# Sparse attention and a rational feed-forward layer on one core: four batches with padded values and DMA transposes, and a new written-out instruction order

## The chip, the core and the metric

The kernel runs on one core of one Trainium2 chip. Its time is device microseconds of one execution. The kernel before has a median of 383.21 us over 9 runs (381.69 to 384.72).

A core has engines that work side by side, each through its own list of instructions in a fixed order: PE (matrix products and transposes into PSUM), DVE (elementwise), ACT (activation functions and copies), POOL (here it issues the DMAs that cast float32 to bfloat16) and SP (issues all other DMAs, among them DMA transposes and the stores of the output). An engine that waits for a semaphore holds up all that is behind it in its list.

## The reference, cut to what matters

```python
def _attn_ref(q, k, v):                       # (8, 8, 576, 64)
    scores = matmul(q, k.transpose(0, 1, 3, 2)) / sqrt(64)
    rel = pos[:, None] - pos[None, :]
    mask_local = (rel >= 0) & (rel < 32)      # heads 0 to 3
    mask_strided = (rel >= 0) & (pos[None, :] % 32 == pos[:, None] % 32)   # heads 4 to 7
    attn = softmax(where(mask, scores, -1e9))
    return matmul(attn, v)

def _moe_ref(x, w_in, w_out, a, b):           # x: (4608, 512), w_in: (512, 2048)
    h = x @ w_in
    P = a[0] + a[1] * h + a[2] * h**2 + a[3] * h**3
    Q = 1.0 + abs(b[0]) * abs(h) + abs(b[1]) * h**2
    return (P / (Q + 1e-6)) @ w_out
```

The attention output, with its heads side by side, is x. Products run in bfloat16 with float32 sums.

## The kernel before, in words

**Attention by batch.** For each of 8 batches q and k are loaded in three parts (`load_qk`, L463: part 0 heads 4 to 7, part 1 heads 0 to 3, part 2 the last 64 positions in a tile tm), and v in three (`load_v`, L484: part 0 VL for the local heads, four DMAs on POOL and two copies on SP; part 1 VT for the strided heads, two DMAs; part 2 VW for the last positions). For batches from 2 on there is one VL, one VT and one VW buffer. They come free (`v_free`) when the last AV tile of the batch before has run.

`scores` (L625) makes, in steps: R1 transposes q and k of the strided heads (16 PE transposes, L680) and DVE copies the result into sT (L683); R2 and R3 do the same for the local heads into kL and qL (ACT); S and L are the scores of the strided and the local heads, whose exponentials ACT writes to ES and EL; TL is a DMA transpose of tm on SP; X holds the scores of the last positions, with exponentials in EX and EW. A branch with `name == "T"` makes sT by four DMA transposes on SP instead of R1, for batches from TB on; TB is 8 here, so no batch takes it.

`attend` (L787) makes five tiles for each batch, T0 to T4. Its matmuls (here called AV, L845) multiply the exponentials by v into 64 columns, and a matmul by ONE, a column of ones, puts the softmax's sum into column 64. For the local heads and VW the ones stand in the value tile itself, in column 64 of runs of VS = 68. DVE then takes the reciprocal of the sum (L853) and scales (L855) into XR. A transpose puts XR into XT, the input of the dense part: for the first four tiles of batches 0 and 1 by PE and a copy (L873, L875), for the others by a DMA transpose on SP (L885).

**Dense part by chunk.** Chunks 0 to 7 are the 512 first positions of each batch, chunk 8 the last 64 of all batches. `dense1` (L907) makes the first product (M1: groups of 8 matmuls 128x512), copies it to HB (ACT, L947), and computes the rational function: DVE L961 to L1012, ACT Ln and Exp (L985, L988) for the division. `dense2` (L1041) makes the second product with Wout (M2: for each chunk two halves, i0 and i1, of four groups of 8 matmuls) and stores. Win comes in four DMAs, Wout in one of 2 MB (L460), all on POOL.

**Order.** Nothing is left to the order of the code. `Program.schedule` (L169) gives each operation the rank that stands for it in the list ORDER, and each engine runs its operations by rank. `emit` puts in the waits. The costs and keys that `add` is given aren't used at run time. Fillers (L584) are matmuls without use, at ranks of their own.

**Batch 0.** Its q, k and v come by DMAs on SP as float32 (`loads0`, L527). DVE and ACT cast them; VL gets its three shifted copies from DVE (L558), ACT (L558) and POOL (L559).

```python
        for eng, o0, i0, n in (("DVE", 64, 64, 64), ("ACT", 32, 64, 32)):
            evl.append(evac(eng, VL[0][o0:o0 + n, 0:8, :, 0:64], stv[i0:i0 + n, :, :, :], [ovs, vi], -960, 2048))
```

Most matmuls are recorded under L597 and most PE transposes under L600, the lines of two helpers (`mm`, `tp`), so a reader goes by tile names.

Of the kernel before, what the change touches and what calls it, by code (L numbers as in the profile page):

```python
# [15 lines left out]
def _bf16_bits(x):  # L16
# [7 lines left out]
    0, 2, 1, 19, 3, 127, 71, 72, 73, 116, 33, 86, 99, 156, 153, 83, 110, 78, 105, 114, 34, 17, 98, 101, 109,  # L24
    12, 103, 36, 140, 82, 53, 108, 117, 97, 61, 25, 43, 118, 100, 50, 18, 112, 26, 60, 48, 29, 87, 55, 32,
    52, 23, 11, 104, 49, 51, 22, 30, 85, 35, 41, 56, 28, 84, 107, 59, 57, 44, 94, 81, 37, 119, 10, 62, 31,
    115, 111, 21, 141, 42, 15, 46, 45, 14, 40, 66, 79, 4, 27, 6, 58, 7, 68, 5, 38, 9, 13, 16, 8, 20, 24, 92,
    91, 93, 102, 77, 90, 132, 139, 65, 54, 39, 122, 47, 126, 63, 69, 70, 113, 75, 160, 158, 147, 154, 157,
    159, 67, 76, 74, 80, 64, 89, 88, 96, 95, 106, 123, 130, 131, 133, 136, 120, 124, 125, 143, 146, 135,
    142, 144, 148, 151, 129, 134, 138, 145, 150, 152, 170, 173, 178, 197, 207, 216, 221, 240, 121, 137, 162,  # L30
    164, 171, 194, 184, 202, 188, 179, 182, 198, 191, 175, 208, 149, 128, 204, 236, 239, 215, 211, 301, 299,
    229, 303, 193, 206, 228, 234, 225, 237, 238, 242, 243, 245, 161, 168, 174, 181, 183, 192, 200, 186, 190,
    195, 196, 203, 210, 155, 163, 165, 166, 169, 213, 232, 172, 176, 189, 217, 231, 241, 177, 187, 167, 180,
    201, 214, 223, 249, 256, 227, 235, 244, 246, 254, 283, 199, 209, 185, 205, 219, 226, 212, 220, 233, 250,
    292, 357, 375, 312, 341, 300, 307, 315, 322, 393, 398, 252, 258, 260, 263, 272, 255, 262, 264, 269, 273,
    265, 270, 274, 278, 280, 257, 268, 277, 281, 285, 230, 267, 275, 302, 287, 324, 333, 337, 343, 224, 222,
    251, 253, 261, 259, 282, 286, 290, 266, 271, 247, 276, 248, 294, 291, 279, 218, 318, 319, 306, 311, 313,
    320, 316, 296, 460, 284, 289, 293, 298, 304, 310, 314, 323, 327, 334, 309, 339, 345, 350, 355, 342, 347,
    348, 354, 353, 359, 360, 363, 365, 369, 370, 374, 373, 376, 378, 380, 381, 389, 390, 400, 288, 295, 297,
    305, 331, 335, 340, 382, 402, 351, 362, 372, 383, 386, 414, 308, 326, 317, 329, 406, 434, 438, 459, 479,  # L40
    448, 468, 494, 498, 514, 518, 330, 371, 356, 366, 377, 388, 384, 395, 410, 418, 426, 436, 503, 472, 521,
    442, 457, 483, 488, 501, 536, 325, 321, 328, 361, 336, 344, 346, 352, 349, 332, 338, 358, 364, 368, 392,
    396, 385, 387, 425, 427, 403, 405, 435, 409, 445, 415, 367, 379, 391, 397, 404, 412, 420, 429, 439, 444,
    394, 421, 451, 466, 464, 449, 452, 453, 458, 461, 463, 465, 469, 470, 473, 475, 478, 477, 480, 482, 484,
    485, 534, 548, 578, 407, 416, 399, 408, 424, 432, 413, 422, 441, 454, 431, 447, 462, 489, 456, 467, 507,
    523, 527, 567, 581, 552, 558, 543, 551, 574, 587, 612, 624, 535, 554, 557, 563, 580, 593, 603, 634, 541,
    549, 555, 559, 562, 615, 597, 599, 608, 568, 576, 590, 598, 604, 701, 669, 703, 670, 411, 428, 401, 455,
    417, 430, 437, 446, 443, 423, 419, 440, 433, 450, 491, 495, 487, 493, 547, 550, 505, 502, 513, 510, 515,
    544, 471, 476, 481, 486, 490, 492, 497, 500, 504, 509, 474, 496, 512, 516, 519, 564, 570, 571, 573, 575,
    577, 579, 611, 583, 589, 591, 594, 595, 600, 601, 605, 606, 655, 660, 693, 506, 511, 517, 528, 532, 546,  # L50
    525, 531, 553, 556, 561, 565, 585, 592, 538, 560, 613, 621, 627, 674, 677, 654, 702, 640, 645, 688, 729,
    713, 734, 635, 656, 663, 675, 694, 709, 717, 744, 609, 618, 628, 643, 662, 672, 762, 691, 668, 667, 679,
    705, 719, 725, 791, 761, 765, 790, 499, 508, 533, 530, 545, 539, 524, 526, 529, 537, 522, 542, 520, 540,
    626, 620, 617, 629, 651, 653, 614, 610, 647, 642, 657, 641, 566, 572, 584, 586, 588, 596, 602, 607, 616,
    619, 582, 623, 625, 630, 632, 676, 681, 683, 686, 687, 690, 692, 697, 698, 706, 708, 721, 711, 715, 716,
    718, 723, 742, 776, 795, 633, 646, 650, 665, 673, 682, 638, 648, 689, 696, 700, 710, 714, 720, 658, 671,
    724, 732, 737, 803, 814, 788, 810, 752, 758, 775, 825, 830, 838, 750, 769, 778, 797, 807, 827, 832, 856,
    730, 740, 755, 764, 785, 789, 802, 823, 826, 793, 813, 821, 831, 835, 839, 899, 842, 907, 569, 637, 631,
    652, 622, 666, 684, 644, 636, 659, 639, 661, 649, 664, 731, 733, 735, 728, 759, 757, 738, 739, 766, 743,
    774, 771, 678, 685, 695, 699, 704, 707, 712, 722, 727, 745, 726, 749, 753, 770, 772, 784, 792, 794, 798,  # L60
    799, 804, 805, 808, 812, 815, 816, 819, 818, 822, 824, 828, 837, 872, 873, 876, 736, 741, 747, 767, 773,
    781, 780, 796, 786, 800, 806, 820, 829, 833, 801, 809, 836, 844, 848, 888, 912, 879, 901, 864, 866, 921,
    929, 933, 942, 862, 875, 880, 892, 913, 925, 930, 946, 846, 858, 870, 877, 886, 904, 905, 900, 898, 889,
    897, 928, 931, 939, 962, 966, 943, 963, 779, 680, 783, 787, 751, 782, 754, 760, 777, 746, 748, 768, 763,
    756, 852, 847, 841, 843, 874, 868, 855, 850, 861, 857, 863, 859, 811, 817, 834, 845, 851, 854, 867, 878,
    881, 883, 869, 884, 887, 895, 910, 885, 890, 891, 893, 894, 902, 903, 916, 906, 909, 911, 914, 918, 922,
    923, 926, 964, 983, 985, 994, 840, 849, 853, 860, 865, 871, 915, 919, 882, 896, 908, 917, 920, 927, 924,
    932, 935, 938, 941, 965, 974, 953, 976, 949, 951, 968, 998, 993, 1002, 947, 954, 957, 969, 973, 979,
    986, 1006, 944, 948, 950, 952, 958, 992, 991, 997, 961, 970, 972, 977, 980, 984, 1015, 987, 1012, 988,
    934, 937, 940, 945, 955, 960, 936, 956, 967, 971, 975, 978, 982, 990, 959, 981, 995, 1000, 1001, 1034,  # L70
    1043, 1020, 1039, 1013, 1017, 1051, 1060, 1026, 1037, 1007, 1021, 1023, 1030, 1036, 1041, 1046, 1067,
    989, 996, 999, 1003, 1005, 1011, 1014, 1009, 1008, 1016, 1019, 1022, 1025, 1028, 1054, 1029, 1033, 1056,
    1004, 1018, 1027, 1032, 1042, 1045, 1010, 1024, 1050, 1055, 1058, 1074, 1085, 1081, 1095, 1062, 1064,
    1080, 1091, 1096, 1100, 1048, 1059, 1065, 1071, 1076, 1082, 1084, 1099, 1110, 1087, 1088, 1105, 1108,
    1112, 1121, 1089, 1093, 1098, 1103, 1104, 1106, 1119, 1113, 1116, 1118, 1130, 1143, 1145, 1035, 1047,
    1094, 1127, 1133, 1137, 1142, 1136, 1139, 1141, 1146, 1148, 1150, 1031, 1038, 1040, 1044, 1049, 1053,
    1073, 1072, 1075, 1052, 1057, 1061, 1063, 1066, 1068, 1077, 1079, 1069, 1070, 1078, 1083, 1086, 1090,
    1124, 1123, 1135, 1126, 1092, 1097, 1101, 1102, 1115, 1132, 1131, 1128, 1120, 1107, 1109, 1111, 1114,
    1117, 1122, 1125, 1129, 1134, 1138, 1140, 1144, 1147, 1149, 1151, 1152, 1153, 1159, 1157, 1156, 1155,
    1154, 1158, 1160, 1162, 1161  # L80
# [203 lines left out]
def bass_strided_sparse_attn__then__act_rational_pade_kernel(nc, q, k, v, moe_w_in, moe_w_out, moe_a, moe_b, out):  # L284
# [12 lines left out]
    HL, DA, TB, NF0 = 4, 1, 8, 70  # L297
# [18 lines left out]
    ES = [A(f"ES{i}", [128, 2, 512], BF) for i in range(NE)]  # L316
    EL = [A(f"EL{i}", [128, 2, 512], BF) for i in range(NE)]
    EX = [A(f"EX{i}", [128, 2, 64], BF) for i in range(NE)]
    EW = [A(f"EW{i}", [128, 12, 2, 32], BF) for i in range(NE)]
# [11 lines left out]
    VL = [A("VL0", [128, 9, 4, VS], BF)]  # L331
    VT = [A("VT0", [128, 4, 256], BF)]
    VW = [A("VW0", [128, 2, VS], BF)]
    t3f = T3[2].rearrange("x f c -> x (f c)")
    VL.append(t3f[:, 0:36 * VS].rearrange("x (m h d) -> x m h d", m=9, h=4))
    VW.append(t3f[:, 36 * VS:38 * VS].rearrange("x (j d) -> x j d", j=2))
    VT.append(t3f[:, 38 * VS:38 * VS + 1024].rearrange("x (h c) -> x h c", h=4))
    NU = 2
    UU = [A(f"UU{i}", [128, G, CH], BF) for i in range(NU)]
    NO = 2  # L340
    OS = [A(f"OS{i}", [128, 2, 512], F32) for i in range(NO)]
    Win = A("Win", [128, NK1, Fmid], BF)
    Wout = A("Wout", [128, NF, Fout], BF)
# [86 lines left out]
    for i in range(NE):  # L430
        memset(EW[i], EW[i].rearrange("x u j c -> x (u j c)"), 0.0, cost=0.5, key=-400 + 200 * i)
# [717 lines left out]
```

The softmax here doesn't subtract the row's maximum and nothing guards it: scores larger than these inputs give would overflow.

## Time and profile before

| what | value |
|---|---|
| median of 9 runs | 383.21 us |
| the profiled execution | 383.18 us |
| its span, first to last instruction | 381.4 us |
| granted PE clock, mean | 0.928 of full |
| dense matmuls 128x512, psO<-Wout | 512, 116.8 us busy in all |
| DVE copies sT<-psS | 8, 1.21 us each |
| matmuls by ONE (ES and EW) | 432 and 128 |
| POOL issues of VT | 12, 0.62 to 2.40 us, median 0.67; landing 4.6 us |
| POOL issues of VL | 24, 0.73 to 2.41 us, median 0.77; landing 3.5 us |
| SP issues of DMA transposes XT<-XR | 24, 1.19 to 4.35 us, median 1.25; landing 2.3 to 14.5, median 3.6 us |

One execution is profiled. Busy time is the time in which an engine runs an instruction; issuing a DMA isn't counted for SP. "Landing" is from the issue to the semaphore. "issue" as a releaser means that the engine waited for nothing that the profile shows. The slices are 40 equal parts of the span of 9.5 us each, with the busy share in tenths. The clock that the throttle grants PE is in tenths too.

### The profile page before, as it was taken

To read this page: it belongs to the slowest core of one execution; us is meant where nothing else is said; L and a number is where in the kernel's file an instruction comes from. 1 tells how busy PE (TensorE), PEld (TensorE's weight loads), DVE (VectorE), ACT (ScalarE), POOL (GpSimd) and SP (SyncE) were. 2 spreads that over 40 slices of the span, in tenths; PEclk is the share of its full clock that TensorE was granted. 3 is DMA by queue.
4 is the path that set the end of the run, shared out by engine and by line. 5 is a ranking of instruction groups with operands and counts; after the bars stand their busy time and mean duration, and the time that the engine had idled before them with its cause. 6 is when DMAs were issued, how large, how long until landed. Compare 5 with 4: busy or idle time off the path is not lost.

```text
span 381.4 us, 10809 instructions
## 1 busy us (share of the span) xinstructions
PE 335.2 (88%) x4902; PEld 178.0 (47%) x4902; DVE 319.6 (84%) x280; ACT 286.6 (75%) x234; POOL 135.2 (35%) x193
## 2 busy tenths in 40 slices
PE   4949948989983699999999999999999999999940
PEld 3733536554452245554555455454444455544410
DVE  0545996979989578899999999999999999999930
ACT  2523792889983598979889999799998899877710
POOL 0893898706935920059308902600000000000000
PEclk9667975999997599999999999999999999999995
DMA  6999899838999960569739694925020331140412
GB/s 208 201 191 151 102 139 88 111 66 87 152 111 160 176 96 2 67 114 138 130 84 94 114 145 90 103 34 116 15 49 8 76 83 29 41 97 1 106 28 87
DMA packets 80254, 37.10 MB, mean 97 GB/s; under 512 B 49360, under 2 KB 75152, under 8 KB 80208
## 3 DMA queue, kind: packets, MB, share of 16 engines
q0 software_dynamic: 48576, 16.79, 41.8%
q1 hardware_dynamic: 31632, 19.62, 24.6%
q8 instruction: 38, 0.62, 0.7%
q14 instruction: 8, 0.07, 0.1%
HBM read 36.90 MB, written 9.44 MB: 121 GB/s over the span
## 4 chain that ended last, share of the span: by engine, by line
PE 81%; DMA 6%; DVE 3%; issue 3%; ACT 3%; SPq 1%; DVEq 0%
PE psO L597 36%; PE psH L597 23%; PE psS L597 12%; PE psA L597 7%; DMA XT<-XR 3%; PE psS L600 2%; DMA HB<-in_k_dram 2%; DVE XR L855 1%; ACT HB L947 1%; ACT VL L607 1%; ACT kL L607 0%; SPq L534 0%; DVE XT L608 0%; DVE OS L1075 0%; DVE sT L608 0%
## 5 line engine op out<-in xcount | busy, mean ns | idle before, releaser
L597 PE MATMUL psO<-Wout,T 128*128 128x512 bf16 x512 | 116.8, 379 | 0.0
L597 PE MATMUL psH<-XT,Win 128*128 128x512 bf16 x336 | 82.8, 389 | 1.6 <-DMA XT<-XR 1.1
L985 ACT ACTIVATE UU<-UU,cst 128x2048 bf16<-128x2048 bf16 (+1 forms) x38 | 72.4, 1913 | 4.4 <-DVE UU L976 4.4
L597 PEld LDWEIGHTS psO<-Wout,T 128*128 128x128 bf16 x512 | 48.8, 98 | 55.8
L988 ACT ACTIVATE UU<-UU 128x2048 bf16<-128x2048 bf16 (+1 forms) x38 | 68.5, 1820 | 0.1
L947 ACT ACTIVATE HB<-psH 128x1024 bf16<-128x1024 f32 x48 | 49.1, 1023 | 19.7 <-PE psH L597 19.3
L597 PEld LDWEIGHTS psH<-XT,Win 128*128 128x128 bf16 x336 | 31.4, 99 | 39.9 <-issue 4.1
L1012 DVE TENSOR_TENSOR T<-T,UU 128x4096 bf16<-128x4096 bf16 (+2 forms) x23 | 41.9, 1821 | 6.6 <-ACT UU L988 6.2
L499 POOL DMA_DIRECT2D VL<-in_v_dram x24 | 23.7, 997 | 56.0 <-PE psA L597 56.0
L976 DVE TENSOR_TENSOR UU<-UU,T 128x4096 bf16<-128x4096 bf16 (+2 forms) x23 | 42.0, 1827 | 0.6
L1002 DVE TENSOR_TENSOR T<-T,HB 128x8192 bf16<-128x8192 bf16 (+3 forms) x17 | 41.0, 2413 | 0.3
L1006 DVE TENSOR_TENSOR T<-T,HB 128x8192 bf16<-128x8192 bf16 (+3 forms) x17 | 41.0, 2412 | 0.3
L961 DVE TENSOR_SCALAR T<-HB 128x8192 uint16<-128x8192 uint16 (+3 forms) x17 | 22.2, 1311 | 5.2 <-ACT HB L947 4.2
L973 DVE TENSOR_SCALAR UU<-T,coef 128x4096 bf16<-128x4096 bf16 (+2 forms) x23 | 25.6, 1115 | 0.7
L597 PE MATMUL psO<-XT,Win 128*128 128x512 bf16 x96 | 24.4, 399 | 1.0 <-DVE XT L608 0.5
L1009 DVE TENSOR_SCALAR T<-T,coef 128x8192 bf16<-128x8192 bf16 (+3 forms) x17 | 23.3, 1372 | 0.2
L478 POOL DMA_DIRECT2D tm<-in_k_dram x32 | 20.3, 639 | 8.5 <-DMA HB<-in_q_dram 8.5
L855 DVE TENSOR_TENSOR XR<-psA,RC 128x512 bf16<-128x512 f32 (+1 forms) x35 | 22.0, 629 | 1.5
L1004 DVE TENSOR_SCALAR T<-T,coef 128x8192 bf16<-128x8192 bf16 (+3 forms) x17 | 22.9, 1345 | 0.3
L995 ACT ACTIVATE T<-HB,coef 128x4096 bf16<-128x4096 bf16 x6 | 22.8, 3794 | 0.0
L1078 ACT ACTIVATE OS<-psO 128x1024 f32<-128x1024 f32 x16 | 16.5, 1031 | 7.8 <-PE psO L597 7.7
L478 POOL DMA_DIRECT2D tm<-in_q_dram x32 | 21.9, 690 | 0.0
(165 smaller groups left out, 499.7 us busy)
## 6 DMA issues: line engine op xcount, KB each, us to landing
out_dram<-OS SPq DMA_DIRECT2D x72, 128.0 KB
kn<-in_k_dram POOLq DMA_DIRECT2D x14, 256.0 KB, 6.2
qn<-in_q_dram POOLq DMA_DIRECT2D x14, 256.0 KB, 6.0
Win<-in_moe_w_in_dram POOLq DMA_DIRECT2D x4, 512.0 KB, 7.5
Wout<-in_moe_w_out_dram POOLq DMA_DIRECT2D x1, 2048.0 KB, 19.4
VL<-in_v_dram POOLq DMA_DIRECT2D x24, 72.0 KB, 3.5
VT<-in_v_dram POOLq DMA_DIRECT2D x12, 128.0 KB, 4.7
HB<-in_k_dram SPq DMA_DIRECT2D x2, 512.0 KB, 6.4
```

Of the source, the lines that this page charges most:

```text
L478: add("POOL", (lambda e, h=h, r0=r0: e.dma_start(tm[r0:r0 + 16, :].rearrange("x (g y d) -> x y g d", g=4, y=2)[:, h % 2], src[b, h, 512:57 ...
L499: add("POOL", (lambda e, h=h: e.dma_start(VL[i][64:128, :, h, 0:64], v[b, h, :, :].rearrange("(m p) d -> p m d", p=64))), [v_free[i], ini[ ...
L597: return lambda e: e.matmul(out_ap, l, r, start=start, stop=stop, skip_group_check=True)
L855: o3 = add("DVE", (lambda d, rc=rc, x=x, src=src, nh_=nh_: d.tensor_tensor(x[:, 0:64 * nh_].rearrange("x (h d) -> x h d", h=nh_), src[:, : ...
L947: o2 = add("ACT", (lambda a, hb=hb, ps=ps, f=f: a.activation(hb[:, f:f + 2, :], ps[:, :, :], AF.Copy)), [o1, old], ca(1024), key.of("HB"))
L973: d2 = add("DVE", (lambda d, u=u, t3=t3, sl=sl, HG=HG: d.tensor_scalar(u[:, 0:HG, :], t3[:, sl, :], b1_ap, b0_ap, op0=Alu.mult, op1=Alu.add)),
L976: d3 = add("DVE", (lambda d, u=u, t3=t3, sl=sl, HG=HG: d.tensor_tensor(u[:, 0:HG, :], u[:, 0:HG, :], t3[:, sl, :], op=Alu.mult)), [d2], ct ...
L985: ln = add("ACT", (lambda a, u=u, zl=zl: a.activation(u[:, zl, :], u[:, zl, :], AF.Ln, bias=cst[:, 0:1], scale=1.0)), [d3, cons], 0.28 + w ...
L988: ex.append(add("ACT", (lambda a, u=u, zl=zl: a.activation(u[:, zl, :], u[:, zl, :], AF.Exp, scale=-1.0)), [ln], 0.21 + w * 0.000833, kz + ...
L1002: d5 = add("DVE", (lambda d, hb=hb, t3=t3, g_=g_: d.tensor_tensor(t3[:, g_, :], t3[:, g_, :], hb[:, g_, :], op=Alu.mult)), [d4], ctt(n), k ...
L1006: d7 = add("DVE", (lambda d, hb=hb, t3=t3, g_=g_: d.tensor_tensor(t3[:, g_, :], t3[:, g_, :], hb[:, g_, :], op=Alu.mult)), [d6], ctt(n), k ...
L1012: d9 = add("DVE", (lambda d, t3=t3, u=u, sl=sl, HG=HG: d.tensor_tensor(t3[:, sl, :], t3[:, sl, :], u[:, 0:HG, :], op=Alu.mult)), [d8, ex], ...
```

## The change

1. **Strided values.** VT becomes 16 x VS wide. For batches 0 to 3 (VSB = 4) it is filled and used as before. For batches 4 to 7 it has column 64 of each run set to one, once, by DVE; it is filled by eight DMAs (one for each head and half) in runs of 64 elements, and one matmul of 65 columns takes the place of the two.
2. **TB goes from 8 to 4**: batches 4 to 7 make sT by four DMA transposes each on SP.
3. **ES and EW** are laid out so that the columns of the four matmuls of a head lie together; the S matmuls write two runs of 32, and ACT writes ES in runs of 32.
4. **First values by DMA.** In `loads0` only DVE casts VL; two DMAs on SP copy it to the other two places. ACT's and POOL's copies go.
5. **Fillers**: 20 of 512 columns (the moving operand is MK) instead of 70 of 128.
6. **ORDER** is another list; the modelled costs given to `add` change too, and have no effect at run time.

```diff
-    HL, DA, TB, NF0 = 4, 1, 8, 70
+    HL, DA, TB, NF0, VSB = 4, 1, 4, 20, 4
...
-    ES = [A(f"ES{i}", [128, 2, 512], BF) for i in range(NE)]
+    ES = [A(f"ES{i}", [128, 2, 8, 2, 32], BF) for i in range(NE)]
...
-    EW = [A(f"EW{i}", [128, 12, 2, 32], BF) for i in range(NE)]
+    EW = [A(f"EW{i}", [128, 2, 12, 32], BF) for i in range(NE)]
...
-    VT = [A("VT0", [128, 4, 256], BF)]
+    VT = [A("VT0", [128, 16 * VS], BF)]
...
+    def vts(i):
+        return VT[i][:, 0:1024].rearrange("x (h c) -> x h c", h=4)
+
+    def vtp(i):
+        return VT[i][:, :].rearrange("x (h g d) -> x h g d", h=4, g=4)
...
         elif part == 1:
...
+            else:
+                if b == VSB:
+                    one.append(add("DVE", (lambda e: e.memset(vtp(i)[:, :, :, 64:65], 1.0)), [v_free[i], one], 0.15, key))
+                for h in range(4):
+                    for c in range(2):
+                        add("POOL", (lambda e, h=h, c=c: e.dma_start(
+                            vtp(i)[64 * c:64 * c + 64, h, :, 0:64],
+                            v[b, 4 + h, 0:512, :].rearrange("(x c g) d -> c x g d", c=2, g=4)[c])),
+                            [v_free[i], one], 0.65, key + 0.01 * h, g, 0.52)
...
-        for eng, o0, i0, n in (("DVE", 64, 64, 64), ("ACT", 32, 64, 32)):
-            evl.append(evac(eng, VL[0][o0:o0 + n, 0:8, :, 0:64], stv[i0:i0 + n, :, :, :], [ovs, vi], -960, 2048))
-        evl.append(add("POOL", (lambda e: e.tensor_copy(VL[0][0:32, 1:8, :, 0:64], stv[96:128, 0:7, :, :])),
-                       [ovs, vi], 3.0, -960))
+        evl.append(evac("DVE", VL[0][64:128, 0:8, :, 0:64], stv[64:128, :, :, :], [ovs, vi], -960, 2048, True))
+        gd = ch_s[0].group()
+        add("SP", (lambda e: e.dma_start(VL[0][32:64, 0:8, :, :], VL[0][64:96, 0:8, :, :])), [evl[0], vi], 0.5, -955, gd, 0.4)
+        add("SP", (lambda e: e.dma_start(VL[0][0:32, 1:8, :, :], VL[0][96:128, 0:7, :, :])), [evl[0], vi], 0.5, -955, gd, 0.4)
...
-    fill = [add("PE", (lambda e: e.matmul(PS["H"][:, 1, 0:128], IDN[:, :], IDN[:, :], start=True, stop=True,
-                                          skip_group_check=True)), [c_idn], 0.1, 9000.0 + z) for z in range(NF0)]
+    fill = [add("PE", (lambda e: e.matmul(PS["H"][:, 1, :], IDN[:, :], MK[:, 0:512], start=True, stop=True,
+                                          skip_group_check=True)), [c_idn, c_mk], 0.216, 9000.0 + z) for z in range(NF0)]
...
+                        if b < VSB:
+                            makers.append(mm(o_[:, 0:64], w, vts(iv)[64 * c:64 * c + 64, h, 64 * g:64 * g + 64], h == 0, True))
+                            makers.append(mm(o_[:, 64:65], w, ONE[64 * c:64 * c + 64, :], False, True))
+                        else:
+                            makers.append(mm(o_[:, 0:65], w, vtp(iv)[64 * c:64 * c + 64, h, g, 0:65], h == 0, True))
```

What the two lists of ranks come to, for the places that matter below (b is the batch, c the chunk; M1 and M2 stand for one group of matmuls each):

```
PE, batch 3 to chunk 3, before:
  ... b4 R1, b3 T3, b4 R2, b3 T4, b4 R3, b4 S, b4 L, c3 M1, b4 X, c3 M1 x4, c0 M2 i0 x2, c3 M1, c0 M2 i0 x2 ...
PE, the same, after:
  ... b3 T3, c0 M2 i0 x2, b4 R2, c0 M2 i0, b3 T4, c0 M2 i0, b4 R3, c3 M1, b4 S, c0 M2 i1, c3 M1 ...
PE, from T4 of batch 4 to T0 of batch 5, before:
  M2, b5 L, M2, b5 X, M2, M1, M1, M2, M1, M1, M2, M1
PE, the same, after:
  M2, M1, b5 L, M2, b5 X, M1, M1, M2, M1, M1
POOL, after: b4 part 0 (k, q), b3's VL and VT, Wout, b3's VW with b4's other q and k, b4's VL, b4's VT x8 ...
POOL, before: b3's VL, b4 k part 1, b3's VT, b3's VW with b4's q and k, Wout, b4's VL ...
POOL, batch 5's values, after: VL x3, VT, VL, one tm load, VT x7
SP, after: b3 T0, T1, T2 (to XT), two transposes to b4's sT, b3 T3 (to XT), two more to b4's sT, TL ...
```

In the new list batch 1's R1, R3, R2, S and L stand among the M1 groups of chunk 0; in the old one they stood behind them.

## The prediction

> **What bounds the kernel now.** I read the page first: the busy shares, then the slices.
>
> ```profile
> PE 335.2 (88%) x4902; PEld 178.0 (47%) x4902; DVE 319.6 (84%) x280; ACT 286.6 (75%) x234; POOL 135.2 (35%) x193
> ...
> PE   4949948989983699999999999999999999999940
> ...
> DVE  0545996979989578899999999999999999999930
> ...
> PEclk9667975999997599999999999999999999999995
> ```
>
> No engine is full over the whole span, but PE (matrix engine) is from slice 13 or so to the end, with DVE just behind. The holes lie in the first third. So I cut the span at the last long PE hole and read both sides in the windows view (busy us and instruction counts by engine, clock, DMA share, GB/s):
>
> ```profile
> 110.00:128.60 18.60, 8.30 (x307) 6.18 (x305) 18.02 (x16) 10.02 (x9) 9.99 (x11) 0.72 1.35 162
> 128.60:366.60 238.00, 237.48 (x2648) 117.02 (x2648) 221.74 (x152) 205.01 (x154) 51.18 (x72) 0.99 0.49 77
> ```
>
> From 128.6 to the last matmul at 366.6 PE waits for nothing (237.5 of 238.0). DVE has 16.3 us of room there. A microsecond of PE work removed in this stretch is one gained; of DVE work, not by itself. In the stretch ahead of it PE idles 10.3 us, with the DMA engines full (1.35). The chain of waits (start, length, what) names what it waits for:
>
> ```profile
> 112.14 1.22 DVE sT L608
> ...
> 113.58 0.69 DVE XR L855
> 114.28 1.20 DVE T L1004
> ...
> 115.79 12.78 DMA XT<-XR
> 128.61 3.52 PE psH L597 x8
> ```
>
> The last DMA transpose of batch 3 (XR to XT) takes 12.8 us where the median lands in 3.6; the 2 MB load of Wout, issued at 107.2 and 19.4 us long, lies over it. Only then can chunk 3's first product begin, at half clock (3.52 us for 8 matmuls against 1.73 later). After the last matmul come 14.8 us of eviction and stores that the change doesn't touch. The span is 381.4, the profiled execution 383.18 us, so 1.8 us lie around the span; the median of the 9 runs is 383.21, the same.
>
> [...] PE stood 3.14 us on "issue" at 22.1. [...] The trace has loads of VT that took POOL 0.62 to 2.40 us each (median 0.67). [...] the queue that POOL feeds shows 48,576 packets for 41.8% of 16 engines, 52 ns each.
>
> **The change part by part.** I sorted both lists of ranks by engine and laid them side by side.
>
> *sT by DMA for batches 4 to 7 (TB 8 to 4).* Gone on PE: 16 transposes a batch, 0.89 to 1.00 us in the chain. Three of the four batches lie after 128.6: 3 x 0.95 = 2.9 us. Gone on DVE: a copy of 1.215 us each; batch 4's is the line at 112.14 above, right in the chain, so the chain is 1.2 us shorter. Added on SP: four DMA transposes a batch, 1.25 us issue each. SP is moved past by them: two stand ahead of batch 3's last XT transpose, so that one comes 2 x 1.25 = 2.5 us later. The S scores must wait for their landing (3.6 median, 14.5 worst); the loads they need are placed well ahead. I take no PE wait for batches 5 to 7; PE's M1/M2 groups hide it.
>
> *Ones column inside V for batches 4 to 7.* 16 one-column matmuls fewer per AV tile. A tile T0 to T3 takes 0.47 us for 48, 9.8 ns each: 16 x 9.8 ns x 16 tiles = 2.5 us. In T4, 32 take 0.53 us (164.71 to 165.24): 16 x 16.5 ns x 4 = 1.1 us. Sum 3.6 us, all after 128.6. The new layout of ES and EW changes no count; its ACT writes now go in runs of 32 elements: 0, at most 4 batches x 2 x 0.1 us on ACT, which has room (205 of 238).
>
> *V in short runs.* VT is loaded by 8 DMAs a batch instead of 2, 4 times the packets: 6 x 0.67 = 4.0 us more POOL issue, and 1536 packets x 52 ns / 16 = 5 us more of every DMA engine, per batch. POOL is idle 65% of the time, but this piece can't start early: there is one VL/VT buffer, free only after the previous batch's T4. I count what PE has between T4 and the next T0 in the new order (an M group of 8 matmuls is 1.73 us): batch 4 19.9 us, batch 5 8 groups + 1.5 = 15.3 us (22.1 us in the trace before), batches 6 and 7 20.5 us each. The chain for batch 5: 4 VL x 0.77 + one tm 0.52 + 8 VT x 0.67 + landing 4.6 = 13.6 us undisturbed. At the VL pace of 201.7 (4.36 us for 4) and VT at 1.0 it is 17.5, so 2.2 late. I take 1 us a batch, 4 us; the bounds are 0 and 23 (below).
>
> *Order.* The new order puts the four product groups c0 M2 i0 (second product of chunk 0, 4 x 1.73 = 6.9 us) between batch 3's last AV and chunk 3's first M1; before, they came after it. So PE fills 6.9 of the 10.3 us hole with work that it did later. They need Wout. POOL issues it right behind batch 3's V loads, at about 94.5 (88.95 + 4.0 + 1.3) rather than 107.2, so it lands near 94.5 + 19.4 = 114; PE gets there near 111 and waits some 3 us, inside the hole. Wout being out of the way, XT should land faster: at best 9.2 us (12.8 to 3.6), at worst not at all, since batch 4's loads still fill the queues. I take 2.0.
>
> *Start and ramp.* Batch 0's VL copies by DMA free ACT of 1.9 us (16.18 to 18.09, in the chain) and POOL of 2.7. They land, after DVE's cast ends near 16 to 17, two issues of 0.6 and some 3 to 4.7 us later: 20 to 22, against 20.1 when the first AV began. Fillers, 20 of 512 columns, fit in waits and drop 100 instructions. Batch 1's attention moves into chunk 0's M1, earlier, so chunk 1 may start earlier but chunk 0's last M1 comes later for DVE. I take 0 for all of it, -4 to +3.
>
> Sum against the profiled 383.2: -2.9 - 3.6 - 1.2 + 2.5 - 6.9 - 2.0 + 4.0 = -10.1, **373.1 us**. DVE after the cut needs 221.7 - 3 x 1.2 = 218 us, PE 237.5 - 6.5 - 6.9 = 224: PE stays the bound, with little to spare.
>
> **The rivals.**
>
> *Better: the hole closes and V is in time.* Chunk 3 then starts when PE is through with c0 M2: 114 + 6.9 + batch 4's R2, R3 and batch 3's T4 (2.5) = 123.4, and 238 - 13.4 = 224.6 us follow: 348 + 14.8 + 1.8 = 364.6. For it: the median landing. Against: DMA at 1.35.
>
> *The hole stays.* XT still lands with Wout or behind the sT transposes, 5 us later than before instead of 0.7 earlier: 373.1 + 5.7 = 379. For it: SP transposes took up to 4.3 us to issue around 107 to 120.
>
> *Slower: V arrives late.* One mechanism: POOL's VT issue in the gap from T4 to T0. The trace has a pair at 166.0 that took 3.79 us, 1.9 each. At that pace the chain is 4 x 1.1 + 0.5 + 8 x 1.9 + 4.6 = 24.7 us, late by 4.8, 9.4, 4.2 and 4.2 = 22.6 us in the four batches; PE, in order, stands. 373.1 + 18.6 = 391.7. It decides from 14 us of lateness in all (4.0 + 10.1), a VT issue of about 1.6 us. Against: the median 0.67.
>
> *It doesn't do what it says.* The rank lists really differ and the edits take effect in the code; what may fail is that the order, made from modelled costs (DMA transposes 1.25 + 0.6 us, against 3.6 landing), isn't the one that the chip rewards. That ends in one of the cases above.
>
> **How the numbers follow.** 373 (369 to 378): 0.50. 365: 0.18. 379: 0.14. 392: 0.18. The range, 363 to 386, leaves out the last. A measurement of this kernel tells about 0.3% (1.1 us) from no change. Faster: 0.50 + 0.18 + 0.10 of the 379 case; same 0.04; slower 0.18.
>
> **What would show it.** Right: no sT copies and no R1 on DVE and PE after batch 3; 432 + 128 one-column matmuls fall by 320; c0 M2 (psO<-Wout) runs between 110 and 125; PE's last hole ends before 129; PE is near full after it. Wrong: waits of PE for VT or VL loads after 130, most at batch 5's T0; waits for sT or XT; DVE idle or PE idle above 5 us after 130; chunk 0's first M1 much later than 29.2.

## The result and the profile after

| | before | after |
|---|---|---|
| median of the runs | 382.80 us (55 runs, 381.25 to 385.46) | 379.58 us (18 runs, 375.76 to 383.04) |
| the profiled execution | 383.18 us | 375.35 us |
| its span | 381.4 us | 373.6 us |
| chunk 0's first product begins | 29.23 us | 37.04 us |
| chunk 3's first product begins | 128.61 us | 128.56 us |
| last matmul ends | 366.58 us | 357.78 us |

The ratio after to before is 0.9892 (0.9872 to 0.9913): 1.1% faster, where 2.6% was forecast. The time lies in the forecast's range, 363 to 386, and the sign is right; the size is not. The runs now spread over 7 us, and the profiled one is the fastest of all, 4.2 us under the median. The trace of after alone therefore flatters the change; two more traces are below. Medians here are over all runs; the ratios leave out the runs that lie over 1.5% above the fastest of their kernel.

The page of after, busy shares and slices:

```profile
PE 322.2 (86%) x4468; PEld 162.2 (43%) x4468; DVE 312.8 (84%) x277; ACT 284.7 (76%) x233; POOL 148.3 (40%) x216
...
PE   0836987499998999999999999999889999999930
...
DVE  0423899989999998899799979997999999999920
```

PE has 434 instructions fewer: 320 ones, 4 x 16 transposes, 50 fillers. DVE's row has 8s and 9s from slice 5 to slice 38, with three 7s, where it had 5 to 7 here and there up to slice 15; PE's hole in slices 13 and 14 is gone. The first four slices have become emptier on both.

The windows view, cut at the same two events as before the change (110 us, chunk 3's first product, the last matmul):

```profile
110.00:128.56 18.56, 17.01 (x339) 8.76 (x336) 18.31 (x18) 16.95 (x12) 2.02 (x3) 1.00 0.56 83
128.56:357.78 229.22, 226.06 (x2356) 108.22 (x2352) 214.22 (x148) 202.73 (x155) 77.58 (x109) 1.00 0.62 89
```

Ahead of the cut PE works 17.0 of 18.6 us, not 8.3, at full clock. Behind it 229.2 us are left of 238.0; the prediction's sum gives 238.0 - 2.9 - 3.6 - 6.9 + 4.0 = 228.6. What PE waits for from 130 us on, in this run (total, times, longest):

```profile
PE psO L613 <- ACT OS L1103: 1.3, 1, 1.3
PE psH L613 <- ACT HB L972: 1.2, 1, 1.2
PE psH L613 <- DMA XT<-XR: 0.6, 1, 0.6
```

No wait for V and none for sT. From chunk 3 on the length is close to the one worked out; whether for the reasons given is taken up below. But chunk 3 doesn't begin earlier, although PE and DVE have no holes ahead of it: the work before it began later. The chain of waits at the start shows where:

```profile
10.10 7.44 DMA T<-in_v_dram
...
17.56 1.24 DVE VL L624
18.81 0.61 SPq L574
...
19.47 4.46 DMA VL<-VL
...
23.97 0.67 PE psA L613 x26
...
27.45 3.93 issue
...
37.16 1.79 PE psH L613 x8
```

The last part of batch 0's v that VL needs lands at 17.54 us (DVE's cast began at 15.94 before), DVE casts it, SP issues two copies, and the second lands at 23.9; the first AV tile (20.1 before) can only then begin. Four tiles later PE stands 3.93 us on "issue", and chunk 0's first product comes at 37 us.

### The profile page after: what moved, and what is told of

The parts are those of the page before. It is cut to its first block, busy times and chain, and to the rows that moved or that the text cites. A ratio compares the mean times of both kernels' runs of the same rounds, so it can differ in the third digit from the quotient of the medians.

```text
span 373.6 us, 9970 instructions
## 1 busy us (share of the span) xinstructions
PE 322.2 (86%) x4468; PEld 162.2 (43%) x4468; DVE 312.8 (84%) x277; ACT 284.7 (76%) x233; POOL 148.3 (40%) x216
## 3 DMA queue, kind: packets, MB, share of 16 engines
q0 software_dynamic: 55104, 16.79, 46.1%
## 4 chain that ended last, share of the span: by engine, by line
PE 64%; DVE 10%; POOL 6%; DMA 6%; SPq 4%; ACT 3%; issue 2%; DVEq 0%
PE psO L613 29%; PE psH L613 18%; PE psS L613 10%; PE psA L613 6%; POOL tm L483 2%; DMA T<-in_v_dram 2%; POOL VT L525 2%; DVE UU L1001 2%; ACT HB L972 2%; DVE XR L880 1%; DVE T L986 1%; DMA XT<-XR 1%; DMA tm<-in_k_dram 1%; DMA VL<-VL 1%; ACT T L1020 1%
## 5 line engine op out<-in xcount | busy, mean ns | idle before, releaser
L613 PE MATMUL psH<-XT,Win 128*128 128x512 bf16 x336 | 79.7, 378 | 3.0 <-ACT HB L972 2.3
L613 PEld LDWEIGHTS psH<-XT,Win 128*128 128x128 bf16 x336 | 30.1, 96 | 39.5 <-ACT HB L972 3.6
L525 POOL DMA_DIRECT2D VT<-in_v_dram x32 | 22.9, 757 | 12.1 <-PE psA L613 12.1
L998 DVE TENSOR_SCALAR UU<-T,coef 128x4096 bf16<-128x4096 bf16 (+2 forms) x23 | 26.5, 1151 | 0.4
L483 POOL DMA_DIRECT2D tm<-in_k_dram x32 | 18.2, 572 | 16.2 <-DMA LT<-tm 9.3
```

The source lines that it names most:

```text
L483: add("POOL", (lambda e, h=h, r0=r0: e.dma_start(tm[r0:r0 + 16, :].rearrange("x (g y d) -> x y g d", g=4, y=2)[:, h % 2], src[b, h, 512:57 ...
L525: add("POOL", (lambda e, h=h, c=c: e.dma_start(vtp(i)[64 * c:64 * c + 64, h, :, 0:64], v[b, 4 + h, 0:512, :].rearrange("(x c g) d -> c x g ...
L613: return lambda e: e.matmul(out_ap, l, r, start=start, stop=stop, skip_group_check=True)
L998: d2 = add("DVE", (lambda d, u=u, t3=t3, sl=sl, HG=HG: d.tensor_scalar(u[:, 0:HG, :], t3[:, sl, :], b1_ap, b0_ap, op0=Alu.mult, op1=Alu.add)),
```

## The experiments

**The changed kernel again, twice**, since its trace was of its fastest run.

> The changed kernel as it is, profiled a second time. Its one trace was of a run of 375.4 us where the median of its runs is 379.6, so about 4 us of the typical run are in no trace yet. Theory: the start made the gain small, so the second trace has chunk 0's first product near 37 us again (29.2 before the change), chunk 3's near 128 to 132, and a length near 380. Theory of lateness (V in short runs or sT by DMA): the extra 4 us are waits of PE (matrix engine) for V or sT after 130 us, in batches 4 to 7. Theory of the start: the extra 4 us are ahead of 130 us, where the loads of all batches crowd.

> The changed kernel a third time, for a trace of a typical run (379 to 380 us). Two traces: 375.4 us, PE waits 4.4 us for the copies of V; 377.5 us, 6.3 us. Theory (the landing of V's loads and copies is what varies): the wait for the copies grows with the time, above 6 us at 379, and chunk 4's first product waits for XT or not. Rival (something after 170 us varies): the same wait for V, and PE idle later.

Medians 378.73 us (6 runs, ratio 0.9875, 0.9828 to 0.9921) and 379.23 (4 runs, 0.9883, 0.9834 to 0.9931). PE's waits from 12 to 36 us, second trace (a run of 377.49 us), then third (378.32):

```profile
PE psA L613 <- DMA VL<-VL: 6.3, 1, 6.3
PE psA L613 <- issue: 3.9, 1, 3.9
```

```profile
PE psA L613 <- issue: 5.0, 1, 5.0
PE psA L613 <- DMA VL<-VL: 4.9, 1, 4.9
```

The two together are 8.3, 10.2 and 9.9 us in the three traces. Chunk 0's first product begins at 37.04, 38.75 and 39.52 us, and the run's time less that start is 338.3, 338.7 and 338.8 us: nearly all of the difference between these runs is made ahead of 40 us. The third run also waits 2.1 us for XT at chunk 4, the first 0.6, the second 0.3. V and sT are in time in all three. So what these two runs add to the first is not lateness of V in batches 4 to 7, but the start. That the wait for the copies alone grows with the time did not hold: it is the sum of that wait and the one on "issue".

**Casts instead of copies by DMA for batch 0**: one part undone.

```diff
-        evl.append(evac("DVE", VL[0][64:128, ...
-        add("SP", (lambda e: e.dma_start(VL[0][32:64, 0:8, :, :], VL[0][64:96, 0:8, :, :])), [evl[0], vi], ...
-        add("SP", (lambda e: e.dma_start(VL[0][0:32, 1:8, :, :], VL[0][96:128, 0:7, :, :])), [evl[0], vi], ...
+        for eng, o0, i0, n in (("DVE", 64, 64, 64), ("ACT", 32, 64, 32)):
+            evl.append(evac(eng, VL[0][o0:o0 + n, ...
+        evl.append(add("POOL", (lambda e: e.tensor_copy(VL[0][0:32, 1:8, :, 0:64], stv[96:128, 0:7, :, :])), ...
```

> The changed kernel with one part undone: batch 0's two copies of V are casts on ScalarE (1.9 us) and GpSimd (2.7 us) again and not DMAs. Theory: PE waited until 23.97 us for the DMAs' landing, the casts end near 20 to 21, so the first AV tile is 3 us earlier and the time 2 to 3 us less, 377. Rival: [...] the first 3 us are lost again by chunk 0's first product: 379.6, the same.

373.98 us (372.52 to 374.76), ratio 0.9747 (0.9711 to 0.9783): 4.75 us under the changed kernel beside it on the same chip, 5.6 under its 18 runs. This version beats both kernels. Its chain at the start:

```profile
18.11 1.02 ACT kL L621
...
19.16 1.91 ACT VL L621
21.09 1.02 ACT ES L739
22.11 0.92 ACT EL L759
...
26.51 2.66 issue
```

The first AV tile begins at 23.13 us, and chunk 0's first product at 34.97, though ACT's cast of 1.9 us is back in the chain. That is 2.1 to 4.6 us earlier than in the three traces of after, and it is kept to the end: the run's time less that start is 338.9 us, again. One reason why the gain is more than my 2 to 3 us is that the wait on "issue" is shorter too: 2.7, not 3.9 to 5.0, so that the two waits of the first AV tiles are 5.2 us together (2.5 for EL) and not 8.3 to 10.2.

**The same part alone in the old kernel.**

> The kernel before with one part of the change alone: batch 0's two copies of V by DMA from SP, behind its start loads, in place of the casts on ScalarE and GpSimd. VectorE's cast ends at 17.2 us there, so the copies land at 22 to 24 and the first AV tile starts 2 to 4 us later than 20.1. Theory that lateness of the start costs its full length in any order: 386 to 388. Theory that it costs only where VectorE or PE is full from there on (the new order) and that the hole ahead of chunk 3 takes it up in the old one: 382 to 384. In both the spread of the runs grows, if the landing of the copies is what varies.

384.22 us, ratio 1.0023 (1.0003 to 1.0043). The trace is of its fastest run (381.47 us). PE waits for the copies here as well:

```profile
PE psS L597 <- DMA VL<-VL: 4.8, 1, 4.8
```

but the wait of 3.1 us on "issue" that the old kernel has at 22.1 us is gone, and so is the 1.4 us for EL. The first AV tile begins at 24.14 us, 4 us late, chunk 0's first product at 30.44, only 1.2 us late, and chunk 2's is not late at all. The range grows from 4.2 to 6.0 us. So by the ratios the same edit costs 0.9 us (0.1 to 1.6) in the old order and 5.6 in the new one. In this trace it is not the hole ahead of chunk 3 that takes most of it up, as I had expected, but the wait on "issue", which is gone when the wait for the copies comes.

**Can the two waits be laid over each other in the new order?** 60 small fillers ahead of everything move the first AV tile in PE's program.

```diff
+    fill += [add("PE", (lambda e: e.matmul(PS["H"][:, 1, 0:8], IDN[:, :], IDN[:, 0:8], ...)),
+             [c_idn], ...) for z in range(60)]
```

> The kernel with batch 0's V cast again (373.98 us), with 60 more small fillers (8 columns) on PE ahead of everything, where PE waits for its first constants anyway. In every trace with an 'issue' hole of 1.2 to 5.0 us in the first AV tiles, it stands at PE's record number 700 (products and weight loads counted together); in the three kernels whose first AV tile began at record 440, the hole was gone when PE waited 4 us there and stayed when it waited 1.5. The 60 fillers move the first AV tile from record 336 to 456. Theory [...]: the hole of 2.7 us shrinks below 1, chunk 0's first product near 32.5, time 372. Rival (the ramp to chunk 1 has another bound, near 71.7 us): hole gone, time 374.

> The changed kernel with the same 60 fillers, the copies of V still by DMA. Theory: [...] the hole of 3.9 to 5.0 us goes, chunk 0's first product near 34 instead of 37 to 39.5, time 375 to 376. Rival [...]: 379, the same.

376.20 us (373.19 to 379.04, ratio 0.9809, 0.9753 to 0.9864) and 380.22 (374.28 to 384.63, too wide for a ratio; its trace is of a run of 381.57 us). No gain in either. A record is one product or one weight load in PE's program, counted from its start. The hole is tied to the record number: it stands at record 701 in both, 120 records earlier in the work than before. But it is still 3.2 us with the casts, and 2.1 with the copies although PE had waited 3.8 us for V at record 456. Both traces also have a hole on "issue" that the others lack, 1.25 and 1.45 us at record 957, and with the casts 1.5 us more at record 457. So the place of the hole is settled and its length is not; my estimates that it would shrink below 1 us with the casts and go with the copies fell.

**More about the start.** ACT's cast moved to DVE; and one more group of chunk 1's second product ahead of chunk 4's first, against the wait for XT.

> The kernel with batch 0's V cast again (373.98 us), but the cast to the second row group on VectorE (1.23 us) and not on ScalarE (1.91 us), where it stood ahead of the exps of batch 0's S and L scores; in that kernel PE waited 2.5 us for the exp of L. Theory: the exps come 2 us earlier, VectorE's last cast of V 1.2 us later, the first AV tile 1 us earlier: 373. Rival: the cast of the strided values on VectorE is now the last: 374 to 375.

> The kernel with batch 0's V cast again (373.98 us), with one more group of chunk 1's second product (1.73 us) ahead of chunk 4's first product. In the traces of the new order, batch 4's last XT transpose takes 4.3 to 8.0 us to land and chunk 4's first product waits for it, up to 3.6 us. Theory (that landing is one of the things that vary): 373 and a range of the runs no wider than 2 us. Rival (in most runs XT is in time, and the group is only moved): 374.

374.96 us (ratio 0.9806, 0.9769 to 0.9842) and 374.52 (0.9783, 0.9745 to 0.9822): no gain in either. In the first, traced in its slowest run (377.92 us), chunk 0's first product begins 1.0 us earlier than with ACT's cast and chunk 1's at 71.66 us, to the hundredth as late. In the second the wait for XT is gone from the trace, which shows 2.2 us with the casts alone; the median doesn't follow. In the traces of the new order that wait is 0.3 to 3.6 us; that it makes the spread was not shown.

**Is it the first part of the new order?** The old order up to chunk 2's first product, then up to chunk 0's only.

```
PE, old order first: b0 T0..T3, c0 M1 f2, f0, f4, b0 X, ..., c1 M1, b3 R1, R2 | from here new: c2 M1 f0, b3 R3, ...
PE, old start only:  b0 T0..T3                                              | from here new: b0 X, b1 R1, c0 M1 f0, f2, b0 T4, ...
```

> The changed kernel, but with the old order of the work on every engine, the old fillers and the old casts of batch 0's V up to chunk 2's first product (92.0 us before, 96.7 after); the new order beyond. Theory (the start ate the gain; from chunk 2 on PE is full): chunk 0's first product at 29 us, chunk 2's at 92, chunk 3's near 124, the time 4 to 5 us under the changed kernel's, 375 in the median. Rival (loads, not the start, set chunk 3): chunk 3's first product stays near 128 with PE waiting ahead of it, time 379 to 380. Rival (the new first part paid for the closed hole): slower than the changed kernel, 382.

> As the last, but the old order ends at chunk 0's first product; batch 0's X scores and batch 1's R1 stay ahead of it as in the changed kernel (2 to 3 us). Theory that the start alone (loads, casts, fillers) is the loss: chunk 0's first product near 32 us, chunk 2's near 92, time 375. Theory that the new ramp between chunk 0 and chunk 2 has a bound of its own (VectorE, loads of batches 1 to 3): chunk 2's first product at 95 or later and 378 to 380.

379.16 us (ratio 0.9878, 0.9847 to 0.9910) and 377.65 (0.9822, 0.9773 to 0.9871). In the first, chunk 0's first product begins at 29.89 us and chunk 2's at 91.67, as hoped, and chunk 3's still not before 130.3: 38.6 us for what takes the new order 31.9. The two orders don't join without a seam (PE waits 4.7 us there for an XR of VectorE), so this is no clean test; but an early start brings nothing by itself, and the theory that the late start alone ate the gain fell with that. In the second PE stood 5.5 us for the tail of k, which batch 0's X needs ahead of chunk 0, so its start was late as well.

Two things set the new first part apart. One is DVE. Busy time from 40 to 132 us (PE, PEld, DVE, ACT, POOL), before and then after:

```profile
40.00:132.00 92.00, 73.11 (x1743) 42.99 (x1741) 80.52 (x92) 67.33 (x66) 63.35 (x89) 0.85 1.05 120
```

```profile
40.00:132.00 92.00, 79.24 (x1705) 42.73 (x1703) 88.89 (x105) 75.43 (x70) 51.37 (x74) 0.96 1.04 123
```

DVE works 80.5 of 92 us in the old order, 82.5 in the kernel with the old first part, 88.9 (97%) in the new one. The other is PE's waits on "issue". They stand in the chain of before, between the first products of chunks 0 and 3, with 5.7 us in all:

```profile
52.48 1.20 issue
...
54.95 2.09 issue
...
60.21 1.00 issue
...
80.47 1.00 issue
...
105.75 0.43 issue
```

In the chain of after PE has 1.4 us of them in that stretch, which is 91.5 us long against 99.4 before. By the chains, 4.3 of the 7.9 us by which it is shorter are waits on "issue" that have gone. Why it has fewer was not tested, and that a full DVE keeps what is lost ahead of it from being made up is a reading, not a test.

**Batch 0's X and batch 1's R1 behind chunk 0's first groups**; the same with the old start; and the old start with GpSimd's loads in the new order.

> The kernel with batch 0's V cast again (373.98 us) and one more part of the new order undone: batch 0's X scores and batch 1's R1 stand behind chunk 0's first two product groups, not ahead of them. Theory (from chunk 0's first VectorE operation on, VectorE and then PE are full, so the end follows that operation by 334 us in every kernel with the new rest): chunk 0's first product 2 to 3 us earlier, near 32, its first VectorE operation near 35, time 371. Rival: the two are needed early for batch 1's attention, and VectorE waits for it later; 374, the same.

> The old start on every engine up to chunk 0's first product (order of loads, fillers, casts of V) with batch 0's X scores and batch 1's R1 behind chunk 0's first two product groups; the new order beyond. In the kernel with the old start and X ahead, PE stood 5.5 us for ScalarE's kL of batch 0's tail ahead of X; that wait should be gone from the path. Theory (end 334 us behind the first VectorE operation of chunk 0): chunk 0's first product near 30, first VectorE operation near 34, time 370. Rival (the ramp needs batch 1's scores early, or their loads): 374 or more.

> An attempt at a version that beats both: the new order with the casts of V, the old order of the start loads and casts on SP, VectorE, ScalarE and PE up to chunk 0's first product (its first AV tile could start at 20 us, against 23 in the kernel with the casts alone), GpSimd's loads in the new order but with batch 1's first V load not ahead of all. Theory (a microsecond of the start, with the new ramp order kept, is a microsecond of time): 371 to 372. Rival (the ramp between chunk 0 and chunk 2 waits for loads or VectorE whatever the start): 374, the same as with the casts alone.

377.31 us (0.9867, 0.9833 to 0.9900), 378.08 (0.9839, 0.9807 to 0.9870) and 378.35 (0.9886, 0.9843 to 0.9929). All slower than the casts alone. Chunk 0's first product begins at 33.11, 29.50 and 33.61 us, earlier than the 34.97 there, and chunk 1's at 73.02, 75.05 and 72.37, later than the 71.66 (the trace of the second is of a run of 381.41 us, 3.3 above its median). In the first, two groups brought forward past X and R1 make chunk 0 begin 1.9 us earlier and chunk 1 1.4 us later. The rule "the end follows the start by 334 us" did not hold in these three. What chunk 1 waits for stands in the chains. With the casts alone:

```profile
67.65 2.30 DVE T L1025
...
69.98 1.29 DVE T L1027
71.27 0.34 DVE XT L622
...
71.66 3.60 PE psO L611 x8
```

In all five traces (these three, ACT's cast and DVE's) the last 8.8 us or more ahead of chunk 1's first product are DVE's alone: it works through chunk 0's rational function, and the copy of batch 1's XT stands behind that in its list. So an earlier chunk 0 helps chunk 1 only if DVE gets through its list earlier. (The section on the change is not exact here: in the old order batch 1's R1 runs at 40.5 us, among chunk 0's groups, and in the new one at 36.1, ahead of them.)

**The order's move alone.** In the kernel before, chunk 0's four groups and Wout are moved ahead.

```
PE:    b3 T3 AV, c0 M2 i0 q0, q4, b4 R2, q8, b3 T4 AV, q12, b4 R3, b4 S, b4 L, c3 M1 f0, ...
POOL:  b3 V, Wout, b4 k, q, ...           then, mended:   b4 k part 0, q part 0, b3 V, Wout, ...
```

> The kernel before with the one move of the order that the prediction counted: the four groups of chunk 0's second product ahead of chunk 3's first, and the load of Wout right behind batch 3's V. The prediction's sum gives 6.9 + 2.0 less, 374. Rival (the hole stays, since XT still lands with Wout or PE now waits for Wout): 379 to 383. Rival (the move shifts the hole to chunk 0's product and costs VectorE time): 383 or more.

> The last kernel again (the kernel before with chunk 0's second product and Wout moved ahead), but with the loads of batch 4's k and q for R1 ahead of batch 3's V and Wout, as in the new order. In the last kernel they stood behind Wout, the q load took 15.7 us to land, and chunk 3's first product came at 132.8 us. The prediction's step: 6.9 + 2.0 less than before, 374, with chunk 3's first product near 126 and PE full from there. Rival (the first part of the old order leaves VectorE and the copies of sT too late, the move alone fills nothing): 381 to 384.

385.45 us (1.0034, 0.9999 to 1.0069) and 383.39 (0.9970, 0.9945 to 0.9996). In the first, traced in a run of 387.56 us, Wout lay ahead of batch 4's q, and the chain has it:

```profile
99.81 15.66 DMA qn<-in_q_dram
```

In the second the groups run from 119.1 us, and chunk 3's first product begins at 133.87: batch 4's scores S and L, with the copies and exponentials of ACT that they wait for, still stand ahead of it, PE stands 2.1 and 2.5 us on "issue" on the way, and DVE works 77.2 of the 92 us. The ratio gives the move 0.3% (0.0 to 0.6); the median of all its runs, 383.39, is not below that of the kernel before beside it, 383.31. So alone it brings nothing that is clear, and not the 8.9 us that I gave it.

**V as before in batches 4 to 7**, with the casts: `VSB` 4 to 8.

> The kernel with batch 0's V cast again (373.98 us) with V in long runs and the ones by matmul in all batches, so without the 320 saved matmuls and without the short runs of batches 4 to 7. Theory (no wait for V in the trace after 130 us, PE full): the ones cost what was worked out before, so 3.6 us slower, 377.5. Theory of the prediction's sum (the short runs cost 4.0 and bring 3.6): 373.6, the same. Theory that V in short runs is late in typical runs: faster, 371 or less.

377.22 us (0.9867, 0.9829 to 0.9904), 3.2 us slower than with the padded V by the medians, which come from two chips, and 4.6 by the ratios. From chunk 3's first product to the last matmul, with the padded V and then without (length, then PE's busy time):

```profile
125.86:356.96 231.10, 226.25 (x2356) 108.32 (x2352) 214.42 (x148) 202.71 (x155) 77.90 (x109) 1.00 0.61 88
127.15:358.83 231.68, 228.65 (x2676) 111.36 (x2672) 214.49 (x147) 202.75 (x156) 63.37 (x85) 1.00 0.60 88
```

The 320 ones take PE 2.4 us there, not the 3.6 worked out. The lengths differ by 0.6 only, as the first trace waits 2.2 us for XT and the second 0.7. The rest of the medians' difference has no source in these traces. No cost of the short runs is seen.

**sT by PE and DVE as before**, with the casts: `TB` 4 to 8, R1 and its copy put in at the places that the old order has them; **and sT by DMA alone in the old kernel**, `TB` 8 to 4.

> The kernel with batch 0's V cast again (373.98 us) with sT of batches 4 to 7 made by 16 transposes on PE and a copy on VectorE again, and without the 16 DMA transposes. Theory: PE and VectorE are both full between 130 and 260 us, so 3 to 4 x 0.95 us on PE or 4 x 1.2 us on VectorE come back: 377 to 379. Rival (the DMA transposes on SP delay the XT transposes and stores, so their removal pays for it): 374, the same.

> The kernel before with sT of batches 4 to 7 by DMA alone, two of batch 4's transposes ahead of batch 3's last XT on SP as in the new order. The prediction's step: -2.9 (PE), -1.2 (the copy in the chain), +2.5 (SP), 381. Theory from undoing it in the new order (12.8 us slower there, though in an order not made for it): 376 or less. Rival (SP and landings delay XT ahead of chunk 3): 384 to 387.

386.79 us (1.0126, 1.0084 to 1.0169), 12.8 us slower than with the DMAs by the medians, 14.5 by the ratios; and 401.57 (1.0489, 1.0455 to 1.0523), 18.3 us slower than the old kernel. PE's waits from 100 us on, with R1 back on PE in the new order:

```profile
PE psS L614 <- ACT EX L793: 4.0, 1, 4.0
PE psS L614 <- ACT HB L970: 2.9, 1, 2.9
```

and from 90 us on with the DMAs in the old order:

```profile
PE psS L596 <- DMA sT<-kn: 15.8, 2, 12.5
PE psA L596 <- DVE XR L854: 7.9, 4, 5.0
```

R1 has a price that I had left out: it needs the PSUM tile psS and then a copy, ahead of everything else that batch's scores do there. The DMAs have one too: SP stands behind stores and V copies, and the longest landing was 12.3 us. Both orders were made for their own form, so neither number is the worth of the edit; they show that this edit can't be moved alone from one order to the other.

## Why the prediction was wrong

*The step that failed: "Start and ramp ... I take 0 for all of it, -4 to +3."* One part of it, batch 0's V copies by DMA, costs 5.6 us in the new order (379.58 against 373.98; 4.75 on the same chip), more than the bound of +3 for the whole. What the sum of 373.1 missed in the three traces of after, in us:

| | 375.35 us | 377.49 us | 378.32 us |
|---|---|---|---|
| chunk 3's first product, worked out at 127.9 (128.6 - 1.2 + 2.5 - 2.0) | +0.7 | +3.2 | +2.7 |
| from there to the last matmul, worked out at 228.6 | +0.6 | +0.8 | +2.1 |
| behind the last matmul, taken as untouched at 16.6 | +1.0 | +0.4 | +0.4 |

The first row is start and ramp together; the ramp won back part of what the start lost. Three things in the working of that step:

- "They land ... 20 to 22, against 20.1": measured 23.9, 26.4 and 25.3 us. SP's new order puts v and constants between each other, so v's last load lands at 17.5 to 18.3 us, and the landing takes 4.5 to 5.8 us, not 3 to 4.7.
- The wait on "issue" behind it was not counted, though the prediction had named it (3.14 us before). In the new order it comes after the wait for V and is 3.9 to 5.0 us long.
- A part that comes out near zero in one order need not do so in another. In the old order it costs 0.9 us, and in its one trace the wait on "issue" is gone when the wait for V comes; in the new order the two follow each other, in all three traces.

*Ones and V: -3.6 and +4.0.* The first has the right sign and is too large: PE's time falls by 2.4. The exponentials that ACT writes to ES in runs of 32 take 1.02 us each, 1.03 before. The second is wrong: POOL's VT issues take 0.757 us on the mean, against the 0.67 to 1.9 that I weighed, and PE never waits for V after 130 us, in any of three traces. The queue that POOL feeds moves 55,104 packets, against 48,576 before: 6,528 more, where 4 x 1536 were worked out. The slower rival, V late, is refuted.

*sT: -2.9, -1.2, +2.5.* No R1 after batch 3, and chunk 3 isn't late through SP. The sizes are open, since undoing the part can't be done without its order (above).

*Order: -6.9 and -2.0.* The groups of chunk 0 run between 118.2 and 125.4 us in the first trace, and the hole is gone, but the hole was misread. These are PE's waits in it before:

```profile
PE psS L597 <- ACT ES L723: 4.6, 1, 4.6
PE psA L597 <- issue: 2.8, 1, 2.8
PE psS L597 <- ACT qL L607: 1.1, 1, 1.1
PE psH L597 <- DMA XT<-XR: 1.1, 1, 1.1
PE psS L597 <- DVE sT L608: 0.7, 1, 0.7
```

XT ended last, but only 1.1 us behind the others, so XT faster alone could bring 1.1 us, not 2.0 and not the 9.2 of the best case. The longest wait, ahead of batch 4's L, is for the exponentials of its S scores. ACT came to them late, as it waited 4.3 us for the transpose of tm (TL), which took 13.3 us to land. The new order puts S and L behind chunk 3's first product (130.4 and 136.3 us, before 120.4 and 126.1), which the sum did not count. The kernel with the groups moved alone leaves them ahead, and its chunk 3 begins at 133.87. Whether moving S and L as well would have closed the hole in the old order was not tested.

That 229.2 us follow where 228.6 were worked out is luck. The 228.6 hold 4.0 us for V, which did not come. In their place PE works some 2 us longer than worked out (226.1 against 224), as S and L now lie behind the cut and the ones bring less, and it stands 3.2 us where it stood 0.5.

*The rival "the hole stays", 379,* has the measured number and the wrong cause: PE doesn't stand for XT ahead of chunk 3. With the casts back the ratio 0.9747 is 373.1 us of 382.8, the forecast's sum, and that too is in part chance: chunk 0 begins 5.7 us later than before, chunk 3 at 125.86 us rather than the 127.9 worked out, and 231.1 us follow to the last matmul rather than 228.6.

*The typical run.* Of the 4.2 us between the traced run and the median, the other two traces show 2.1 and 3.0: 1.7 and 2.5 at the start, 0.4 and 0.5 behind it. There is no trace of a run above 378.4 us with the change unaltered, so the last microsecond stays open.

## What to carry to other kernels

A part that costs nearly nothing in one order must be priced again in the order that it will run in: the same two copies cost 0.9 us where the wait on "issue" went when theirs came, and 5.6 where the wait on "issue" followed theirs. A hole must be read wait by wait: the one that ended last here was worth 1.1 of 10.3 us. A copy between two parts of SBUF that stands at the head of the chain was cheaper here on an engine (1.9 and 2.7 us) than by DMA (4.5 to 5.8 us to land) while the loads ran. Where an order is written out by hand, the edits and the order are one change: parts tried alone in the old order cost 0.9, about 0 and 18 us here, so their prices don't add.

## What the runs showed of the hardware

PE's longest hole on "issue" in the start is tied to a place in its program: record 699 to 701, products and weight loads counted together, in the 18 of 20 traces that have it, with 60 fillers ahead or without, and it is 1.2 to 5.0 us long. It was missing in the two traces in which PE waited over 4 us at record 440, and still there in those with waits of 3.8 to 6.3 us at records 336 and 456. Further holes on "issue" stand in steps from there: at 957 in two traces, and in before at 1713 (2.06 us), 1969 (1.00), 2731 (1.00), 3747 (0.43) and 4257 (2.75). The distances are 256, or two, three or four times 253 to 255. (Not all holes fit: one of 1.2 us at 1509 does not.) In the three traces of after none of those between 957 and 2731 is over 0.25 us. What makes these holes, and what sets their length, was not found.

Landing times vary: the last XT transpose of batch 4 lands in 4.2 to 8.0 us in the 14 traces that have the new order from chunk 3 on and sT by DMA, and the copies of V in 4.5, 5.8 and 5.5 us in three runs of one kernel. After, with two such landings in its chain, spreads by 7 us where before spreads by 4; that the landings make the spread was not shown, and with the casts and the 60 fillers, without the copies, six runs still spread by almost 6 us.
